# Key weights loaded second, behind one x tile; fold map built on GpSimd; first products and den/num products in parts; all engines' orders laid anew

## The chip, the cores and the metric

The kernel runs on one core of a Trainium2 chip. A core has TensorE (PE in the profile; PEld are its weight loads), VectorE (DVE), ScalarE (ACT), GpSimd (POOL) and SyncE (SP), which here only issues DMAs. The metric is the device time of one execution in microseconds, taken as the median of several runs.

## What is computed

x is 2048 tokens by 640, in bf16. First comes a linear attention of 32 heads of 20 columns, then an MLP, both with a layer norm ahead and a residual sum behind:

```python
qkv = (layernorm(x) @ wqkv)...            # q, k, v: (B, H, S, 20)
pq, pk = q @ w_phi[h], k @ w_phi[h]       # per head, 20 x 20
phi_q = concat([softmax(pq), softmax(-pq)])
phi_k = concat([softmax(pk), softmax(-pk)])
kv = einsum("bhsf,bhsd->bhfd", phi_k, v)
z  = phi_k.sum(over s)
o  = (phi_q @ kv) / (phi_q . z + 1e-6)
h  = x + o.reshape(B, S, D) @ wo
h2 = h + silu(layernorm(h) @ w1) @ w2     # w1: 640 x 1728, w2: 1728 x 640
```

## The kernel before

The tokens lie in 16 tiles of 128 (t = 0 to 15). The kernel has no loop that is seen in the trace: every step is a function `op_...` that issues a few instructions on one engine, and a long text, `ORDER` (lines 25 to 66), names the steps one after another. A word such as `vc.3.a` calls `op_vc(3, "a")`; the ending `.v`, `.a`, `.p` or `.s` names VectorE, ScalarE, GpSimd or the DMA queue of SyncE. Each engine carries out its own words strictly in the order of the text, and waits before each for the data and the buffers that it needs. So the text is at the same time the queue of each engine.

The steps, with the lines of the profile:

- Loads: `lx.a.b` (tiles a to b of x), `lk.a.b` (chunks of 128 rows of the key weights), `lv` (value weights), `lp` (w_phi), `lq.c` (query weights, transposed by DMA into the buffer of the key weights, once those have been read), `lo`, `l1`, `l2`, `lh` (wo, w1, w2). All but `lp` are issued by SyncE.
- Folding w_phi into the weights: `wt.c` transposes a chunk of the key weights on PE (L300), `wc.c` copies it out of PSUM; `mk` and `ph` (L187 to 193) spread w_phi over a mask to the block map `phb`; `fk.c` multiplies the two on PE (L315), `fc.c` copies out chunk c of the folded key weights `Wfk`. `gk` and `gc` do the same for the query weights `Wfq`.
- Layer norm of a tile: `st` (L258, L259, statistics on DVE), `rs` (L263, L264, the reciprocal root on GpSimd, for one or more tiles), `rm` (a bias for ScalarE), `xn` (the normalised tile: L275 on DVE, L280 on ACT). Then the transpose `XnT`: for tiles 0 to 3 `xt` on PE (L286) with the copy `xc`, for all others `xd`, a transposing DMA (L293).
- Key side: `kp` (L343, ten matmuls of the tile with `Wfk`), `ke` (L365, two exponentials on ACT), `kr` (L373 row sums and L376 reciprocal on DVE), `ka` (L381, the normalisation of 1280 columns on GpSimd; `ka.t.h` does half and `kb` the other half on DVE). Value side: `vp` (L343, ten matmuls) and `vc` (copy to `Vp`). `cc` (L403, 20 small matmuls) adds the tile to kv and z, which stay in one PSUM buffer up to `km` (L413).
- Query side, for groups of four tiles: `qp` (L423, ten or five matmuls of 512 columns) and `qe` (L433, exponentials).
- After `close`, per tile: `dp` (L457, numerator and denominator), `dw` (L470 to L477) and `dr` on DVE, `do` (L492, two halves, on DVE or GpSimd), `td` (transposing DMA to `ot`), `op` (L519, times wo), `oa` (L528, residual), `sq`, `sa`, `sr`, `hn` (second layer norm), `hd` (transposing DMA), `up` (L593, L603) and `ua` (SiLU), `yp` and `yh` (L639, L654), `yo`, `so` (output).
- `wm` is a matmul of zeros whose result nobody reads; eight stand ahead of the text, four more in it (L252).

PSUM gives four buffers, `mm`, for all products and PE transposes; kv holds one of them from the first `cc` to `km`. The exponentials `Ek` have eight buffers, the normalised tiles `xn` seven, the value tiles `Vp` ten.

Of the kernel before, what the change touches and what calls it, by code (L numbers as in the profile page):

```python
# [47 lines left out]
dw.8.v do.6.1.p do.6.0.p sr.2 td.6 op.9 hn.5 ua.0.2 sa.3 hn.2 dr.10 sa.4 hd.2 do.10.1.v dp.7 sr.4
dr.8 yp.0.0 oa.9 hd.5 dw.7.v sa.9 sq.9 do.8.0.p yp.0.1 sr.3 do.10.0.v sr.9 yh.0.0 dr.7 td.10 dp.11
yo.0 do.8.1.p yp.1.0 hn.4 dw.11.v hd.4 yp.1.1 td.8 hn.3 dr.11 op.6 hd.3 yo.1 dp.13 oa.6 op.8 dw.13.v  # L50
op.10 hn.9 up.1.1 oa.10 oa.8 dr.13 sa.8 sq.8 up.1.2 do.7.1.v do.11.1.p do.11.0.v sq.6 do.7.0.p sr.8
td.7 up.1.6 ua.1.2 do.13.1.p hn.8 td.11 ua.1.1 do.13.0.v dp.15 ua.1.6 so.0 up.1.3 dw.15.v td.13 hd.8
dp.12 ua.1.3 dr.15 op.7 hd.9 dw.12.v up.1.5 oa.7 dr.12 sa.7 sq.7 up.1.0 do.12.1.v do.15.0.p ua.1.5
sr.7 sa.6 hn.7 up.1.4 ua.1.0 sa.10 do.12.0.p sr.6 td.12 op.11 ua.1.4 op.13 oa.11 do.15.1.v yp.4.1
oa.13 td.15 hn.6 hd.6 yh.1.0 dp.14 yp.4.0 dw.14.v hd.7 yp.2.0 dr.14 do.14.1.v yo.4 op.15 up.2.2
oa.15 up.2.1 ua.2.2 sq.11 yp.2.1 op.12 up.2.4 oa.12 do.14.0.v sa.12 yo.2 sa.11 td.14 up.2.5 so.4
up.2.3 ua.2.5 ua.2.4 ua.2.1 up.2.0 ua.2.3 sq.10 up.2.6 ua.2.0 sq.15 yh.1.1 op.14 sq.13 sq.12 yp.3.1
oa.14 ua.2.6 sa.14 sq.14 sr.10 yp.7.1 sa.15 hn.10 sa.13 yp.3.0 sr.13 sr.11 yp.5.0 sr.15 hn.11 hd.11
sr.14 yp.5.1 sr.12 hn.14 hd.14 yp.9.0 yo.5 hn.13 so.2 hd.10 yp.9.1 hd.13 yo.3 yp.6.0 hn.12 so.1
hn.15 hd.15 yp.7.0 so.3 so.5 hd.12 yp.8.0 yh.2.1 yh.2.0 yo.9 yp.8.1 yo.7 yp.6.1 up.4.0 yo.6 so.6  # L60
up.3.0 ua.4.0 yo.8 so.8 up.4.2 so.7 so.9 up.4.3 up.3.6 ua.4.3 up.3.1 ua.3.6 ua.4.2 ua.3.0 up.3.3
up.3.2 up.4.1 ua.3.2 ua.3.1 up.3.5 ua.4.1 ua.3.3 up.3.4 ua.3.5 yp.15.1 ua.3.4 yh.4.0 yh.3.0 yp.15.0
yp.10.1 yo.15 so.15 yp.12.0 yp.14.1 yp.12.1 yp.14.0 yp.10.0 yo.14 so.14 yp.11.1 yo.10 yo.12 so.12
yh.3.1 yp.11.0 yq.13.0 yo.11 so.11 so.10 yq.13.1 yz.13.0 yz.13.1 sz.13.0.a sz.13.1.s
"""

@with_exitstack
def kernel(
# [103 lines left out]
    def tok(Xt, t):  # L172
        return Xt[:, :, (t % GT) * P : (t % GT + 1) * P]
# [10 lines left out]
            base=DH, pattern=[[-d, C], [DH, 8]], channel_multiplier=-1,  # L184
        )

    def op_ph():  # L187
        nc.vector.tensor_tensor(
            phb[:],
            phr[:].unsqueeze(2).to_broadcast([P, C, 8, DH]),  # L190
            mask5[:].unsqueeze(3).to_broadcast([P, C, 8, DH]),
            op=ALU.mult,
        )
# [56 lines left out]
    def op_wm(n=512, ps=None):  # L250
        ps = mm2() if ps is None else ps
        nc.tensor.matmul(ps[:, 0, 0:n], warm[:, 0:P], warm[:, 0:n], start=True, stop=True)  # L252
        return ps
# [82 lines left out]
            tl["gk", ce][:, :, 0:320].rearrange("p a (r k) -> p a r k", r=C),  # L336
        )

    def proj(t, W):
        ps = mm2()  # L340
        for half in range(2):
            for c in range(C):
                nc.tensor.matmul(  # L343
                    ps[:, half, 0:320], tok(XnT[t // GT], t)[:, c, :], W[:, c, half * 320 : (half + 1) * 320],
                    start=(c == 0), stop=(c == C - 1),
                )
# [4 lines left out]

    def op_vc(t, eng="a"):
        copy(
# [2 lines left out]
            tl["vp", t][:, :, 0:320].rearrange("p a (h f) -> p a h f", f=DH),  # L356
        )

    def op_kp(t):
        tl["kp", t] = proj(t, Wfk)  # L360

    def op_ke(t):
        Ek = first.tile([P, 2, D], BF16, name="Ek", bufs=8)
# [83 lines left out]
        for lo in (0, FH):  # L447
            dma(q, w2[lo : lo + FH, FC, :], B_w2[FC * P : F, :])

    def op_dp(t):  # L450
        g, i = t // GT, t % GT
        ps = [mm2(), mm2()]
        for s in range(2):
            for r in range(C):
                for a in range(2):
                    lo = 64 * a
                    nc.tensor.matmul(  # L457
                        ps[s][:, a, HQ[r] * 22 : (HQ[r] + 4) * 22],
                        EqT[g][lo : lo + 64, s, r, i * P : (i + 1) * P],
                        KVBD[lo : lo + 64, s, r, :, :].rearrange("p j c -> p (j c)"),  # L460
                        start=(r == 0),
                        stop=(r == C - 1),
                        skip_group_check=True,
                    )
# [251 lines left out]
```

## Time and profile before

| | |
|---|---|
| median of 3 runs | 243.91 us (243.8 to 245.86) |
| profiled execution | 244.62 us |
| its span, first to last instruction | 242.3 us |
| granted PE clock | 1.000 |
| ACT busy | 100.0 us (41%) |
| GpSimd busy | 85.5 us (35%) |
| DMA | 20.59 MB, mean 85 GB/s |

The span is what the profile shows; the execution's own time is 2.3 us longer, for what lies around the first and last instruction. "Busy" counts an engine's time inside instructions. A row of the timeline or the chain begins with its start in us from the beginning of the span and its length in us; a name such as `Ek<-Ek,Sk` is output and inputs; what stands in brackets at the end of a row is how long the engine sat idle ahead of it, and what released it. In a row by groups, "x16 | 23.3, 1453" is 16 instructions, 23.3 us in all, 1453 ns each. Matmuls are pipelined, so that rows that overlap are longer than what PE spends on them.

### The profile page before, as it was taken

Reading aid. Unit: us, or ns where it says so; the run is one execution under the profiler, and the core shown is the slowest. Engines: PE = TensorE matmul, PEld = TensorE weight load, DVE = VectorE, ACT = ScalarE, POOL = GpSimd, SP = SyncE. Lnnn points to the kernel's source line nnn. Section 1 sums busy time; section 2 is a strip of 40 time slices with the busy share of each in tenths; the row PEclk is TensorE's granted clock in tenths of the full one; section 3 lists DMA queues with packets and bytes.
Section 4 is the critical chain, followed back from the end, with each engine's and each line's share of the span. In section 5 each row is a group of like instructions: output and inputs, shape, how many; then the busy total and the mean of one; then the engine's idle time right before and its main releaser. Section 6 shows DMA issues by size and latency. Waiting matters only on the chain.

```text
span 242.3 us, 5172 instructions
## 1 busy us (share of the span) xinstructions
PE 233.0 (96%) x2144; PEld 150.0 (62%) x2160; DVE 142.2 (59%) x266; ACT 100.0 (41%) x149; POOL 85.5 (35%) x160
## 2 busy tenths in 40 slices
...
DMA packets 42806, 20.59 MB, mean 85 GB/s; under 512 B 34336, under 2 KB 42272, under 8 KB 42784
## 3 DMA queue, kind: packets, MB, share of 16 engines
...
q10 hardware_dynamic: 800, 0.16, 0.4%
...
## 4 chain that ended last, share of the span: by engine, by line
PE 79%; DVE 14%; DMA 4%; issue 1%; POOL 1%; ACT 0%; DVEq 0%; ACTq 0%
PE mm L639 24%; PE mm L593 23%; PE mm L519 9%; PE mm L423 8%; PE mm L343 7%; DVE Sk L373 4%; DVE stats L258 3%; PE mm L457 3%; DMA XnT<-xn 2%; DVE xn L275 2%; PE mm L403 2%; DMA X<-in_A_x_dram 1%; DVE Ek L381 1%; PE mm L654 1%; PE mm L603 1%
## 5 line engine op out<-in xcount | busy, mean ns | idle before, releaser
L639 PE MATMUL mm<-w,shT 128*128 128x320 bf16 (+2 forms) x415 | 58.2, 299 | 0.1
L593 PE MATMUL mm<-HnT,w 128*128 128x512 bf16 (+1 forms) x317 | 57.7, 336 | 0.4
L615 ACT ACTIVATE shT<-mm 128x1024 bf16<-128x1024 f32 (+2 forms) x29 | 27.0, 964 | 61.6 <-PE mm L593 55.9
L639 PEld LDWEIGHTS <-shT 128*128 128x128 bf16 x416 | 39.7, 98 | 17.4 <-issue 0.8
L593 PEld LDWEIGHTS <-w 128*128 128x128 bf16 x325 | 31.2, 98 | 23.8 <-issue 0.2
L343 PEld LDWEIGHTS <-XnT 128*128 128x128 bf16 x320 | 30.6, 98 | 15.5 <-DMA XnT<-xn 3.2
L662 DVE TENSOR_TENSOR ob<-mm,X 128x640 bf16<-128x640 f32 x15 | 12.1, 818 | 45.6 <-PE mm L639 36.9
L381 POOL TENSOR_TENSOR Ek<-Ek,Sk 128x1280 bf16<-128x1280 bf16 (+1 forms) x16 | 36.8, 2321 | 4.5 <-DVE Sk L376 4.2
L528 DVE SCALAR_TENSOR_TENSOR X<-mm,X 128x640 bf16<-128x640 f32 x16 | 13.0, 819 | 23.0 <-PE mm L519 22.8
L433 ACT ACTIVATE EqT<-mm 128x1024 bf16<-128x1024 f32 (+1 forms) x24 | 19.7, 880 | 13.7 <-PE mm L423 13.7
L343 PE MATMUL mm<-Wfk,XnT 128*128 128x320 bf16 x160 | 23.6, 300 | 1.4 <-DMA XnT<-xn 1.4
L343 PE MATMUL mm<-wv,XnT 128*128 128x320 bf16 x160 | 23.4, 299 | 1.4 <-DMA XnT<-xn 1.2
L365 ACT ACTIVATE Ek<-mm 128x640 bf16<-128x640 f32 x32 | 20.8, 711 | 9.3 <-PE mm L343 8.0
L373 DVE TENSOR_REDUCE Sk<-Ek 128x64 f32<-128x1280 bf16 x16 | 23.3, 1453 | 2.1 <-ACT Ek L365 2.1
L519 PE MATMUL mm<-wo,ot 128*128 128x320 bf16 x160 | 23.7, 300 | 0.0
L423 PE MATMUL mm<-XnT,Wfq 128*128 128x512 bf16 x93 | 23.1, 380 | 0.4
L541 POOL TENSOR_SCALAR HM<-HST 128x1 f32<-128x1 f32 x16 | 3.7, 232 | 52.2 <-DVE X L528 52.2
L536 ACT ACTIVATE sq<-X 128x640 bf16<-128x640 bf16 x16 | 11.8, 738 | 21.9 <-DVE X L528 20.0
L519 PEld LDWEIGHTS <-ot 128*128 128x128 bf16 x160 | 15.3, 98 | 6.9 <-issue 0.3
L492 POOL TENSOR_TENSOR o<-u,rd 128x320 bf16<-128x320 f32 x19 | 13.9, 742 | 13.8 <-DVE rd L486 7.7
L423 PEld LDWEIGHTS <-Wfq 128*128 128x128 bf16 x100 | 9.2, 98 | 10.0
L258 DVE BATCH_NORM_STATS2 stats<-X 128x6 f32<-128x320 bf16 x32 | 13.6, 467 | 3.0 <-DMA X<-in_A_x_dram 3.0
...
## 6 DMA issues: line engine op xcount, KB each, us to landing
...
```

Of the source, the lines that this page charges most:

```text
L258: nc.vector.bn_stats(stats[:, k, :], X[:, t, k * 320 : (k + 1) * 320])
L343: nc.tensor.matmul(ps[:, half, 0:320], tok(XnT[t // GT], t)[:, c, :], W[:, c, half * 320 : (half + 1) * 320], start=(c == 0), stop=(c == C ...
L365: nc.scalar.activation(Ek[:, s, :].rearrange("p (a n) -> p a n", a=2), tl["kp", t][:, :, 0:320], AF.Exp, scale=1.0 - 2.0 * s,)
L373: nc.vector.tensor_reduce(Sk[:], tl["ek", t][:].rearrange("p s (h f) -> p (s h) f", f=DH), axis=AX.X, op=ALU.add,)
L381: eng.tensor_tensor(Ek3, Ek3, tl["sk", t][:, lo:hi].unsqueeze(2).to_broadcast([P, hi - lo, DH]), op=ALU.mult,)
L423: nc.tensor.matmul(ps[:, k, :], Wfq[:, c, r * P : (r + 1) * P], XnT[g][:, c, :], start=(c == 0), stop=(c == C - 1),)
L433: nc.scalar.activation(E[:, s, rs[0] : rs[-1] + 1, :], tl["qp", g, i][:, 0 : len(rs), :], AF.Exp, scale=1.0 - 2.0 * s,)
L492: (nc.vector if eng == "v" else nc.gpsimd).tensor_tensor(tl["o", t][:, a * 320 : (a + 1) * 320].rearrange("p (h f) -> p h f", f=DH), tl["u ...
L519: nc.tensor.matmul(ps[:, half, 0:320], tl["ot", t][:, c, :], wo[:, c, half * 320 : (half + 1) * 320], start=(c == 0), stop=(c == C - 1),)
L593: nc.tensor.matmul(ps[:, i * W : (i + 1) * W], w1[:, c, fc * P : (fc + 1) * P], HnT[g][:, c, 0:W], start=(c == 0), stop=(c == C - 1), skip ...
L615: nc.scalar.activation(sh[:, a:b], tl["up", g, k][:, 0 : b - a], AF.Silu)
L639: nc.tensor.matmul(ps, shT[g][:, fc * W + i * P : fc * W + (i + 1) * P], w2[:, fc, a:b], start=first and fc == 0, stop=last and fc == FC - ...
```

## The change

- The loads begin with one tile of x (tile 3) in place of two; the key weights follow in the order 2, 1, 4, 0, then tile 2 of x, then key chunk 3. All loads of x are issued ahead of the first `xd`; `lo`, most of `l2`, `l1` and `lq` have other places.
- `ph` runs on GpSimd, ahead of `rs.3`.
- `kp` and `vp` can be issued in parts, over chunks lo to hi of the 640 rows: for tiles 2 and 3 in two parts each.
- `dp` is issued in halves, for s = 0 and s = 1, and takes one PSUM buffer each.
- Six warm-up matmuls ahead of the text in place of eight, two in it in place of four.
- The order of all words is another. All sixteen `st` stand ahead of the first `kr`. All sixteen `ka` run whole on GpSimd; there is no `kb`. All sixteen `vc` are on ACT (before, three on DVE), `xn` is on ACT for four tiles (before, two), `fc` on ACT for all five chunks. `qp.1.0` stands ahead of the last `cc`. Behind `close`, 23 half tiles of `do` are on GpSimd (before, 19).

The diff, with the order up to the words behind `close`, and its last line:

```diff
-lp.a lx.2.4.s ta lk.0.1.s lk.1.2.s mk lk.3.4.s lk.2.3.s lk.4.5.s lx.1.2.s lx.0.1.s st.3 lv.3.5.s
-lx.4.8.s st.2 wm.512 wm.256 wt.1 lv.0.3.s wt.3 wc.1.a ph rs.2.2 wt.0 wc.3.a wt.2 wc.0.v fk.1 wt.4
-wc.2.v fc.1.a fk.0 xn.2.v lq.2 fk.2 wc.4.v fc.0.a fk.3 xn.3.v fk.4 fc.2.a fc.3.v xt.3 lq.4 fc.4.a
-wm.256 xt.2 xc.3.v xc.2.a st.0 wm.512 kp.3 lq.3 st.1 rs.0 kp.2 lq.1 xn.0.v rs.1 st.5 lx.8.12.s xt.0
-ke.2 vp.3 xn.1.v st.4 xc.0.a vp.2 st.7 vc.3.a rs.4.2 st.6 xt.1 vc.2.a vp.0 xc.1.a xn.5.v rs.6.2 kr.2
-xd.5 gk.2 vc.0.a kp.0 mo gc.2.a ke.3 xn.6.v vp.1 xn.4.v ka.2.p xd.6 st.9 ke.0 kp.5 st.10 xd.4 xn.7.v
-gk.3 lx.12.16.s ke.5 st.8 vp.5 xd.7 st.11 gc.3.a kp.1 lq.0 vc.5.a kr.0 rs.8.4 vp.4 rm.8 st.15 ka.0.p
-vp.6 vc.4.a st.12 ke.1 kp.7 st.13 xn.8.a mc kp.4 xn.9.v vc.6.a xd.8 xn.11.v vc.1.a st.14 gk.1 xd.9
-ke.4 kp.6 kr.3 rs.12.4 gc.1.a l2.0.4.s vp.7 xd.11 ke.7 xn.12.v ka.3.p kr.5 vp.8 l1.0.s vc.7.a ke.6
-gk.0 xn.15.v vp.9 rm.14 xn.10.v ka.5.p gc.0.a kr.4 vc.8.a gk.4 kp.9 gc.4.a xn.13.v ka.4.p kr.6 xd.13
-cc.0 cc.2 ke.9 cc.3 l2.4.8.s cc.5 xd.10 kp.11 vc.9.a ka.6.p kr.9 xn.14.a lh.s qp.0.2 ke.11 xd.14
-kr.7 kp.8 l1.2.s xd.12 qp.0.0 ke.8 kr.1 ka.7.p xd.15 qe.0.2 vp.13 kr.11 qe.0.0 l2.8.13.s lo.s ka.1.p
-l1.1.s kp.13 kr.8 kp.14 ka.11.p cc.6 ke.14 cc.7 cc.1 ka.8.h cc.4 vc.13.a kr.14 kp.10 ke.13 kp.12
-ke.10 kr.13 ka.14.p kp.15 ke.12 kr.10 qp.0.1 ka.9.p ke.15 kb.10 vp.14 qe.0.1 kb.8 ka.10.h kr.15
-vp.11 ka.13.p vc.14.a vp.15 vc.11.v kr.12 ka.15.p vp.10 vc.15.a vp.12 vc.10.v ka.12.p cc.13 vc.12.v
-cc.10 cc.9 cc.8 cc.14 cc.15 cc.11 cc.12 qp.1.2 km.0 close km.1 dp.1 qe.1.2 qp.1.0 dw.1.v dp.0 qe.1.0
-dr.1 qp.1.1 dw.0.v do.1.0.p dp.3 qe.1.1 dr.0 qp.3.0 dw.3.v do.0.1.p do.1.1.p do.0.0.p td.1 dp.4
-qe.3.0 dr.3 qp.2.1 dw.4.v td.0 dp.5 do.3.1.v qe.2.1 qp.2.0 do.3.0.v dr.4 dw.5.v do.4.1.p do.4.0.p
-op.1 qe.2.0 td.4 dr.5 op.0 oa.1 td.3 sa.1 dp.2 oa.0 do.5.0.p qp.2.2 dw.2.v sa.0 sq.0 do.5.1.p qp.3.2
-qe.2.2 sr.0 td.5 op.4 qe.3.2 dr.2 do.2.1.v do.2.0.p sq.1 dp.9 oa.4 td.2 op.3 sr.1 hn.0 hd.0 hn.1
...
-yh.3.1 yp.11.0 yq.13.0 yo.11 so.11 so.10 yq.13.1 yz.13.0 yz.13.1 sz.13.0.a sz.13.1.s
+lp.a lx.3.4.s ta lk.2.3.s lk.1.2.s mk lk.4.5.s lk.0.1.s ph.p lx.2.3.s st.3 lk.3.4.s wt.2 lx.0.2.s
+lv.0.3.s wt.1 rs.3 wc.2.v lv.3.5.s wt.4 wc.1.v wt.0 lx.4.8.s mc wc.4.a fk.2 xn.3.v lx.8.12.s fk.1
+wc.0.v fc.2.a st.2 wm.512 fk.0 fc.1.a wt.3 xt.3 fc.0.a lq.1 wc.3.v fk.4 rs.2 xc.3.v wm.256 fk.3
+fc.4.a kp.3.0.3 xn.2.v fc.3.a lq.2 st.0 xt.2 kp.3.3.5 xc.2.a lx.12.16.s st.1 vp.3.0.3 ke.3 kp.2.0.3
+rs.0.2 kp.2.3.5 xn.0.v vp.2.0.3 ke.2 xn.1.v st.5 xt.0 vp.2.3.5 xc.0.a st.4 vp.3.3.5 xt.1 kp.0 st.6
+xc.1.a rs.4.2 vc.2.a vp.1 xn.5.v xn.4.v xd.5 st.7 vp.0 vc.1.a st.8 xd.4 rs.6.2 vc.3.a gk.2 st.11
+vc.0.a rm.7 kp.1 lq.0 ke.0 st.9 lq.4 vp.5 ke.1 st.10 xn.6.v vp.4 xn.7.a rs.8.4 st.12 xd.6 vc.5.a
+st.13 kp.5 mo vc.4.a xd.7 gc.2.a st.14 kp.4 ke.5 lo.s rm.9 xn.11.v st.15 gk.4 xn.9.a gk.0 kr.3 kp.6
+rs.12.4 gc.4.a xd.9 ke.4 vp.6 rm.14 lq.3 rm.13 xn.8.v ke.6 ka.3.p kr.1 vp.7 xd.11 gc.0.a gk.1 xd.8
+xn.12.v vc.7.a ka.1.p kp.7 kr.2 xn.14.a xd.12 vc.6.a vp.9 xn.13.a xn.15.v ka.2.p kr.0 gc.1.a kp.9
+xd.13 vc.9.a ke.7 vp.11 xd.15 xn.10.v ka.0.p kr.5 l2.4.8.s cc.1 l1.2.s cc.3 vc.11.a l2.0.4.s cc.2
+kr.6 xd.14 ke.9 gk.3 ka.5.p kp.8 gc.3.a lh.s vp.13 kr.7 ke.8 l1.1.s ka.6.p xd.10 kp.12 vc.13.a kr.4
+vp.12 ka.7.p kr.9 kp.15 vc.12.a ke.12 ka.4.p kp.13 kr.8 kp.11 ka.9.p kr.12 cc.5 cc.6 ke.15 cc.7 cc.0
+cc.4 ka.12.p ke.11 kr.15 kp.14 ke.13 vp.15 kr.11 ka.15.p ke.14 vp.14 vc.15.a kr.14 vp.8 ka.8.p kp.10
+vc.8.a kr.13 ka.14.p qp.0.0 ke.10 vc.14.a kr.10 qp.0.2 ka.13.p qe.0.0 vp.10 qe.0.2 ka.11.p qp.1.0
+vc.10.a qp.0.1 ka.10.p qe.1.0 cc.15 qe.0.1 cc.9 cc.12 cc.11 cc.14 cc.13 cc.8 cc.10 qp.1.2 km.0 close
+km.1 dp.1.0 qe.1.2 dp.1.1 qp.1.1 dw.1.v dp.0.0 qe.1.1 dp.0.1 dr.1 qp.2.1 dw.0.v dp.3.0 qe.2.1 dp.3.1
+dr.0 qp.3.0 dw.3.v do.0.1.p do.0.0.p td.0 dp.5.1 qe.3.0 dp.5.0 dr.3 qp.2.0 dw.5.v l1.0.s do.3.0.p
+do.1.0.p do.3.1.p do.1.1.p dp.4.0 td.3 qe.2.0 dp.4.1 dr.5 op.0 dw.4.v do.5.0.p td.1 do.5.1.p qp.2.2
+oa.0 dp.2.1 qe.2.2 dp.2.0 dr.4 qp.3.2 dw.2.v do.4.1.p sq.0 do.4.0.p op.1 qe.3.2 sa.0 td.4 sr.0
...
+yp.11.1 yh.3.1 yq.13.0 yo.11 yo.10 so.11 so.10 yq.13.1 yz.13.0 yz.13.1 sz.13.0.s sz.13.1.a
@@ 
             base=DH, pattern=[[-d, C], [DH, 8]], channel_multiplier=-1,
         )
 
-    def op_ph():
-        nc.vector.tensor_tensor(
+    def op_ph(eng="v"):
+        (nc.vector if eng == "v" else nc.gpsimd).tensor_tensor(
             phb[:],
             phr[:].unsqueeze(2).to_broadcast([P, C, 8, DH]),
             mask5[:].unsqueeze(3).to_broadcast([P, C, 8, DH]),
@@ 
             tl["gk", ce][:, :, 0:320].rearrange("p a (r k) -> p a r k", r=C),
         )
 
-    def proj(t, W):
-        ps = mm2()
+    def proj(key, t, W, lo, hi):
+        if lo == 0:
+            tl[key, t] = mm2()
+        ps = tl[key, t]
         for half in range(2):
-            for c in range(C):
+            for c in range(lo, hi):
                 nc.tensor.matmul(
                     ps[:, half, 0:320], tok(XnT[t // GT], t)[:, c, :], W[:, c, half * 320 : (half + 1) * 320],
                     start=(c == 0), stop=(c == C - 1),
                 )
-        return ps
-
-    def op_vp(t):
-        tl["vp", t] = proj(t, wv)
+
+    def op_vp(t, lo=0, hi=C):
+        proj("vp", t, wv, lo, hi)
 
     def op_vc(t, eng="a"):
         copy(
@@ 
             tl["vp", t][:, :, 0:320].rearrange("p a (h f) -> p a h f", f=DH),
         )
 
-    def op_kp(t):
-        tl["kp", t] = proj(t, Wfk)
+    def op_kp(t, lo=0, hi=C):
+        proj("kp", t, Wfk, lo, hi)
 
     def op_ke(t):
         Ek = first.tile([P, 2, D], BF16, name="Ek", bufs=8)
@@ 
         for lo in (0, FH):
             dma(q, w2[lo : lo + FH, FC, :], B_w2[FC * P : F, :])
 
-    def op_dp(t):
+    def op_dp(t, s):
         g, i = t // GT, t % GT
-        ps = [mm2(), mm2()]
-        for s in range(2):
-            for r in range(C):
-                for a in range(2):
-                    lo = 64 * a
-                    nc.tensor.matmul(
-                        ps[s][:, a, HQ[r] * 22 : (HQ[r] + 4) * 22],
-                        EqT[g][lo : lo + 64, s, r, i * P : (i + 1) * P],
-                        KVBD[lo : lo + 64, s, r, :, :].rearrange("p j c -> p (j c)"),
-                        start=(r == 0),
-                        stop=(r == C - 1),
-                        skip_group_check=True,
-                    )
-        tl["dp", t] = [p[:, :, 0:352].rearrange("p a (h c) -> p a h c", c=22) for p in ps]
+        ps = mm2()
+        for r in range(C):
+            for a in range(2):
+                lo = 64 * a
+                nc.tensor.matmul(
+                    ps[:, a, HQ[r] * 22 : (HQ[r] + 4) * 22],
+                    EqT[g][lo : lo + 64, s, r, i * P : (i + 1) * P],
+                    KVBD[lo : lo + 64, s, r, :, :].rearrange("p j c -> p (j c)"),
+                    start=(r == 0),
+                    stop=(r == C - 1),
+                    skip_group_check=True,
+                )
+        tl.setdefault(("dp", t), {})[s] = ps[:, :, 0:352].rearrange("p a (h c) -> p a h c", c=22)
 
     def op_dw(t, eng="v"):
         A = tl["dp", t]
@@ 
     ops = {k[3:]: f for k, f in locals().items() if k.startswith("op_")}
     with tc.manual_schedule(engines={PE, SP, POOL, DVE, ACT}):
         ps = None
-        for i in range(8):
+        for i in range(6):
             ps = op_wm(512, ps)
         for word in ORDER.split():
             name, *args = word.split(".")
```

More of the change, by code (lines that the diff above doesn't have):

```diff
@@ L42 @@
-dr.1 qp.1.1 dw.0.v do.1.0.p dp.3 qe.1.1 dr.0 qp.3.0 dw.3.v do.0.1.p do.1.1.p do.0.0.p td.1 dp.4
-qe.3.0 dr.3 qp.2.1 dw.4.v td.0 dp.5 do.3.1.v qe.2.1 qp.2.0 do.3.0.v dr.4 dw.5.v do.4.1.p do.4.0.p
-op.1 qe.2.0 td.4 dr.5 op.0 oa.1 td.3 sa.1 dp.2 oa.0 do.5.0.p qp.2.2 dw.2.v sa.0 sq.0 do.5.1.p qp.3.2
-qe.2.2 sr.0 td.5 op.4 qe.3.2 dr.2 do.2.1.v do.2.0.p sq.1 dp.9 oa.4 td.2 op.3 sr.1 hn.0 hd.0 hn.1
-qp.3.1 oa.3 hd.1 dw.9.v sq.3 op.5 qe.3.1 op.2 oa.5 sa.5 dp.10 oa.2 up.0.0 dr.9 dw.10.v do.9.0.p sa.2
-up.0.3 ua.0.0 do.9.1.v dp.6 sq.4 td.9 up.0.1 dw.6.v sq.5 ua.0.3 sr.5 sq.2 dp.8 dr.6 ua.0.1 up.0.2
@@ L48 @@
[L48 to L63, printed above, removed]
-yh.3.1 yp.11.0 yq.13.0 yo.11 so.11 so.10 yq.13.1 yz.13.0 yz.13.1 sz.13.0.a sz.13.1.s
+lp.a lx.3.4.s ta lk.2.3.s lk.1.2.s mk lk.4.5.s lk.0.1.s ph.p lx.2.3.s st.3 lk.3.4.s wt.2 lx.0.2.s
@@ new lines @@
+dr.0 qp.3.0 dw.3.v do.0.1.p do.0.0.p td.0 dp.5.1 qe.3.0 dp.5.0 dr.3 qp.2.0 dw.5.v l1.0.s do.3.0.p
+do.1.0.p do.3.1.p do.1.1.p dp.4.0 td.3 qe.2.0 dp.4.1 dr.5 op.0 dw.4.v do.5.0.p td.1 do.5.1.p qp.2.2
+oa.0 dp.2.1 qe.2.2 dp.2.0 dr.4 qp.3.2 dw.2.v do.4.1.p sq.0 do.4.0.p op.1 qe.3.2 sa.0 td.4 sr.0
+dp.9.1 dr.2 dp.9.0 oa.1 op.3 td.5 hn.0 sa.1 sq.1 dw.9.v do.2.1.p hd.0 qp.3.1 sr.1 hn.1 op.4 oa.3
+qe.3.1 hd.1 sa.3 op.5 do.2.0.p oa.4 td.2 sq.4 dp.10.0 dp.10.1 up.0.1 dw.10.v l2.8.13.s op.2 dr.9
+ua.0.1 dr.10 do.9.1.p oa.5 do.10.0.p up.0.3 oa.2 do.9.0.v dp.6.1 ua.0.3 dp.6.0 dp.8.1 sq.3 dw.6.v
```

17 lines of the change are left out of this document (added).

## The prediction

> **What bounds the kernel now.** I read the page's busy line first, then busy time by stretch, the list of waits, and the chain of waits.
>
> ```profile
> PE 233.0 (96%) x2144; PEld 150.0 (62%) x2160; DVE 142.2 (59%) x266; ACT 100.0 (41%) x149; POOL 85.5 (35%) x160
> 0.00:72.46 72.46, 67.23 (x781) 47.01 (x784) 62.87 (x106) 44.85 (x69) 49.62 (x61) 1.00 0.69 173
> 72.46:239.02 166.56, 165.77 (x1364) 102.97 (x1378) 79.06 (x160) 55.17 (x80) 35.91 (x99) 1.00 0.26 47
> 239.02:242.30 3.28, 0.00 (x0) 0.00 (x0) 0.27 (x1) 0.00 (x0) 0.00 (x0) 1.00 0.17 50
> ```
>
> The columns of the last three rows are the stretch, its length, then PE, PEld, DVE, ACT and POOL busy. I cut at 72.46, where the last kv product (`cc`) ends. Behind it PE lacks 0.8 us in 166.6: there is nothing to win there, only to lose. Ahead of it PE lacks 5.2, and part of its 67.2 is warm-up. So what the change can win lies ahead of 72.46. The two longest waits there, for a transpose `XnT`, are quoted further down; the next one:
>
> ```profile
> PE mm L403 <- DVE Vp L158: 0.6, 1, 0.6
> ```
>
> ```profile
> 0.79 3.37 DMA X<-in_A_x_dram
> ...
> 17.60 1.41 DVE Sk L373
> ...
> 24.90 5.96 DMA XnT<-xn
> ...
> 33.80 0.32 PE mm L315 x6
> ...
> 40.18 1.36 PE mm L343 x10
> 41.53 1.65 PE mm L403 x80
> ...
> 69.59 2.86 PE mm L403 x140
> ...
> 73.63 0.50 PE mm L457 x20
> ...
> 85.18 2.27 PE mm L423 x10
> ```
>
> The chain (start, length, what) runs through DVE up to 24.9, over one slow transpose to 30.9, then over PE, over DVE and GpSimd again from about 53 to 69.6, and over PE to the end. It also gives PE's prices: a `kp` or `vp` 1.36, a `gk` or a PE transpose 0.32, a `cc` 1.65/4 = 0.41, a `dp` 0.5, a `qp` of ten 2.27 (of five 1.14).
>
> **The new order, engine by engine.** Everything is carried to one point, the end of the last `cc`, since what PE does behind it stays the same but for one `qp`, which moves ahead of it.
>
> DVE first, since all 16 `st` now stand ahead of the first `kr`, and every `ka` waits for a `kr`.
>
> ```profile
> L258 DVE BATCH_NORM_STATS2 stats<-X 128x6 f32<-128x320 bf16 x32 | 13.6, 467 | 3.0 <-DMA X<-in_A_x_dram 3.0
> L259 DVE BATCH_NORM_AGGREGATE MV<-stats 128x2 f32<-128x12 f32 x16 | 3.3, 208 | 0.6
> L158 DVE COPY wTk<-mm 128x640 bf16<-128x640 bf16 x3 | 1.4, 482 | 0.0
> L373 DVE TENSOR_REDUCE Sk<-Ek 128x64 f32<-128x1280 bf16 x16 | 23.3, 1453 | 2.1 <-ACT Ek L365 2.1
> L376 DVE RECIPROCAL Sk<-Sk 128x64 f32<-128x64 f32 x16 | 8.8, 553 | 0.6
> L188 DVE TENSOR_TENSOR phb<-phr,mask 128x800 bf16<-128x800 bf16 x1 | 1.0, 952 | 0.0
> L158 DVE CAST Wfk<-mm 128x640 bf16<-128x640 f32 x1 | 0.8, 819 | 0.0
> ```
>
> ```profile
> L275 DVE TENSOR_SCALAR xn<-X,MV,RS x8: 394/444/2469, 8.1 to 24.5; 128x640 bf16<-128x640 bf16 x8
> ```
>
> A `st` is 16.9/16 = 1.06, a copy 0.48, a normalisation `xn` 0.44 (median), a `kr` 1.45 + 0.55 = 2.0. Trial on the old queue: 8 `st`, `ph`, 4 copies, 1 cast and 5 `xn` give 14.35; it took 17.60 - 4.16 = 13.4, since neighbours overlap, so I scale by 0.94. The new queue ahead of the first `kr`: 16 `st` 16.9, 5 copies 2.4, 8 `xn` 3.5: 22.8, scaled 21.4. `ph` (0.95), the cast `fc.3` and, later, three casts of `Vp` and two half tiles `kb` have left DVE.
>
> Start: one x tile, half the bytes, in place of two.
>
> ```profile
> 5.35 0.45 PE L300 MATMUL mm<-ident,wk 128*128 128x128 bf16 x5
> ```
>
> Between the landing at 4.16 and this first transpose two key chunks land, as many bytes as the two tiles, in 1.2. The one tile lands between 3.6 (if half of that goes) and 4.16 (if it is all latency); I take 3.9.
>
> Waits that this order adds. GpSimd does `ph` as soon as its operand has landed, and `rs.3` stands behind it; `xn.3` on DVE waits for `rs.3`, with `wc.0`, `st.2` and the rest queued behind.
>
> ```profile
> phr<-in_A_w_phi_dram ACTq DMA_DIRECT2D x1, 25.0 KB, 3.7
> ```
>
> ```profile
> L381 POOL TENSOR_TENSOR Ek<-Ek,Sk x16: 1267/2356/2933, 19.7 to 69.0; 128x1280 bf16<-128x1280 bf16 x14, 128x640 bf16<-128x640 bf16 x2
> ```
>
> ```profile
> 15.39 0.23 POOL L263 TENSOR_SCALAR RS<-MV 128x2 f32<-128x2 f32 x1 [1.79 <-DVE MV L259]
> 15.71 0.71 POOL L264 TENSOR_TENSOR RS<-RS,nhalf 128x2 f32<-128x2 f32 x1
> ...
> 38.30 7.15 POOL L381 TENSOR_TENSOR Ek<-Ek,Sk 128x1280 bf16<-128x1280 bf16 x3
> ```
>
> The operand is there at 0.79 + 3.7 = 4.5. `ph` on GpSimd is not in the trace; its 800 elements cost between DVE's 0.95 and a full `ka`'s 2.36; on the line through the half tile (1.27) and the full one (2.36) 1.54, which I take: 6.05. `rs.3` takes at most what the form for two tiles takes, 1.03 (15.39 to 16.42): 7.1. DVE is there at 3.9 + 1.06 + 0.96 = 5.9, so it waits 1.2. Next, `rs.0.2` takes tiles 0 and 1 together and waits for `st.1`, and `xn.0` stands right behind `st.1`: 1.03 and a hand-over, 1.1 more, with `rs.4.2` queued behind it. First `kr`: 3.9 + 21.4 + 2.3 = 27.6.
>
> GpSimd: `kr.3` to 29.6, `xn.8` to 30.0, then 16 full `ka` back to back. Three in a row took 7.15, so 2.38 each: 38.1, to 68.1. Three more `xn` stand among them. That the two engines shut each other out is in the rows:
>
> ```profile
> 19.73 2.61 POOL L381 TENSOR_TENSOR Ek<-Ek,Sk 128x1280 bf16<-128x1280 bf16 x1
> 20.06 2.47 DVE L275 TENSOR_SCALAR xn<-X,MV,RS 128x640 bf16<-128x640 bf16 x1
> ```
>
> An `xn` of 0.4 lasted 2.47, until the `ka` was over. The Trainium skill (SBUF — State Buffer, Terms, on the shared port pair) says the same: an exclusive lock held for the whole instruction, the loser fully blocked. By that rule `ph` would hold up only an `xn`, and none is due while it runs; the sum stays. Each `xn` thus holds up the next `ka` by 0.4: 1.2 in all, so GpSimd ends at 69.3 and the last `cc` could end at 69.8.
>
> PE: the first product needs `xc.3`. DVE: `xn.3` to 7.5, `wc.0`, `st.2`, `wc.3`, `xc.3` (0.48 + 1.06 + 0.48 + 0.48, scaled 2.4) to 9.9. So 10.0 in place of 10.58:
>
> ```profile
> 10.58 2.88 PE L343 MATMUL mm<-Wfk,XnT 128*128 128x320 bf16 x20
> ...
> 26.66 2.89 PE L343 MATMUL mm<-wv,XnT 128*128 128x320 bf16 x20 [1.15 <-DMA XnT<-xn]
> ...
> 30.91 2.89 PE L343 MATMUL mm<-Wfk,XnT 128*128 128x320 bf16 x20 [1.35 <-DMA XnT<-xn]
> ```
>
> From there to the last `cc`: 32 products 43.5, 5 `gk` 1.6, 3 transposes 1.0, 16 `cc` 6.6, three `qp` of ten and one of five 7.9: 60.6. The same count for the old order (two transposes, two `qp` of ten and one of five) is 58.0, with its waits (1.15 + 1.35 + 0.6) 61.1, against 61.9 measured, so 0.8 of small ones goes on top: 10.0 + 61.4 = 71.4. PE is later than GpSimd by 1.6, so PE sets the point.
>
> Does PE run dense? The transposes it waited for: the old `xd.7` (issued at 24.9) stood behind a 640 KB load of x, which now stands ahead of all `xd`. `xd.5` follows `xn.5`: DVE has done 7 `st`, 5 copies and 5 `xn` (12.0, scaled 11.3) and both waits by 17.5, say 17.7. Landing is 4.3 median:
>
> ```profile
> XnT<-xn SPq DMA_TRANSPOSE x12, 4.3
> ot<-o SPq DMA_TRANSPOSE x16, 2.6
> ```
>
> so it is there at 22.0; PE, with eight products, three transposes and a `gk` (12.2) behind 10.0, comes to `vp.5` at 22.2. `xd.4`, 1.2 later, is needed 1.36 later. No slack, but no queue ahead either: 0 to 1.7 us of wait (at 6.0, the longest landing), I take 0.1. `xd.9` now stands behind the 800 KB of `wo` on SP, and its `xn.9` on ACT behind `ke.5`, which needs `kp.5` (26.3); PE comes to `vp.9` five products and three `gk` later, at 34.1, so 7.8 for ACT's work (some 3) and a landing of 4.3. The weight loads now ahead of `xd.14` and `xd.10` are covered by the seven products, a `gk` and five `cc` ahead of `kp.14` (11.9); if that cover is gone, PE waits there, with `qp` behind. ACT takes on about 4 us (three casts of `Vp`, two `xn`), with 27 free. For all these I put 0.3, so the last `cc` ends at 71.7. The split products add no instruction; `dp` in halves takes one buffer at a time, a gain of nothing where PE didn't wait. Two warm-ups fewer at the head cover a shorter start.
>
> Sum: 71.7, then what stood behind 72.45 in the old span (169.85) less the one `qp` (2.27): 239.3, which is 3.0 under 242.3. By the profiled execution 244.62 - 3.0 = 241.6; the median of the runs stood 0.7 lower, at 243.91, so 240.9.
>
> **Rivals.** *Slow start of the matmuls.* Rows first:
>
> ```profile
> 1.24 4.23 PE L252 MATMUL mm<-warm 128*128 128x512 bf16 x10 [1.24 <-DVE warm L130]
> ...
> 6.03 1.01 PE L300 MATMUL mm<-ident,wk 128*128 128x128 bf16 x15 [0.23 <-DMA wk<-in_A_wqkv_dram]
> ```
>
> A warm-up of 512 columns takes 0.42, a `qp` matmul of 512 columns 0.227: PE starts at half pace, though the granted clock reads 1.00. By 6.03 fifteen of 128 columns take 1.01: full pace, with 4.1 us of warm-ups ahead of the first transpose. Six warm-ups end at 1.24 + 2.5 = 3.8, and PE then has transposes, small products and holes up to 10.0. If the pace is still half there, it takes another 4.1 us of products to lift it, at a loss of 2.05: 242.95 (two such spells: 245.0). For it: the shorter head. Against: the old trace holds its pace from 5.35 to 10.58 with small work too. The Trainium skill (TensorE: Matmul & The Clock Gate, Part 1) has the gate opening after a busy window of about 3.4 us, and Part 4 has transposes not counted as busy in the same way, which speaks for this rival; the rows leave it open. Chance 0.13.
>
> *The cover behind `close` is missed.* `qp.1.0` filled 2.27 there. The new order reaches `op.0` after five `dp` and four `qp`, 2.5 + 9.1 = 11.6. Its `ot` needs `dp.0` (3.3), DVE's `dw` and `dr`, two `do` and a transpose of 2.6:
>
> ```profile
> 77.08 0.29 DVE L470 RECIPROCAL w<-mm 128x32 f32<-128x32 f32 x1
> ...
> 79.70 0.36 DVE L470 RECIPROCAL w<-mm 128x32 f32<-128x32 f32 x1
> ...
> 79.84 2.10 POOL L492 TENSOR_TENSOR o<-u,rd 128x320 bf16<-128x320 f32 x3 [1.65 <-DVE rd L486]
> ```
>
> 3.3 + 2.6 + 1.4 + 2.6 = 9.9, so 1.7 are spare. If that fails, the stage gives back at most what the filler covered, 2.27: 243.1. Chance 0.12.
>
> *The transposes come late again*, with another queue ahead: 2.5 of wait stay, 243.3. Chance 0.07.
>
> *GpSimd becomes the bound: slower.* Its `ka` start at 30.0, ten later than now, and nothing is left out between them. If a tile costs 2.93, the longest row, the last ends at 30.0 + 46.9 + 1.2 = 78.1, the last `cc` at 78.5; against 72.45 + 2.27 = 74.7, the point of no gain, 3.8 late: 247.7. It decides against the change from (74.7 - 0.4 - 31.2)/16 = 2.69 a tile. For it: it has little slack, 1.6 against PE. Against: `kr` ran beside the three at 2.38. Chance 0.14.
>
> **The numbers.** Forecast 240.9, chance 0.54, its own range 239.0 (no new waits, an earlier x tile, `ph` at DVE's price: 1.9 better) to 242.4 (1.5 of wait at the transposes). A measurement here tells about 1% (2.4 us) from no change. Under 241.5: most of the forecast's case, 0.5. Over 246.3: most of the GpSimd case, 0.13. Between: 0.37, the other three and the rest of these two. The range goes from 239.0 to 245.3: it takes in the three middle cases and leaves out most of the slower one and the forecast's lower edge.
>
> **What would show it.** `ph` at about 4.5 for 1.5 on GpSimd and `xn.3` waiting for it; the first product at 10.0; no PE wait over 0.5 between 20 and 35; the first `ka` near 30, sixteen to about 69; the last `cc` near 71.7 with a fourth `qp` ahead of it; PE dense behind. Wrong: products at 0.27 a matmul after 10.0, PE waiting for `ka` at the end, or for `ot` behind `close`.

## The result, and the profile after

The changed kernel takes 240.93 us (median of 4 runs, 240.85 to 240.95), the one before, run beside it, 243.87. The ratio is 0.9853, with a 95% interval from 0.9804 to 0.9902: about 1.5% faster. The two medians alone differ by 2.9 us, 1.2%, which lies inside that interval. The forecast was 240.9.

Busy line of the page, and busy time by stretch (stretch, length, then PE, PEld, DVE, ACT and GpSimd), cut at the first product of a tile with folded weights and at the end of the last `cc`:

```profile
PE 232.8 (97%) x2140; PEld 151.5 (63%) x2156; DVE 130.6 (55%) x254; ACT 104.4 (44%) x154; POOL 90.8 (38%) x167
0.00:11.18 11.18, 8.93 (x69) 6.25 (x69) 5.22 (x14) 4.54 (x7) 6.39 (x24) 1.00 0.82 260
11.18:71.47 60.29, 60.24 (x724) 43.26 (x722) 48.56 (x85) 45.70 (x70) 45.31 (x40) 1.00 0.60 134
71.47:235.70 164.23, 163.27 (x1349) 101.76 (x1365) 76.08 (x155) 54.19 (x78) 39.07 (x103) 1.00 0.27 58
```

The span is 239.0, 3.3 less. The middle row is the whole result: from the first product at 11.18 to the last `cc` at 71.47 PE lacks 0.05 us. Before, it lacked 3.4 from 10.58 to 72.46 and had one query product less to do. From the last `cc` to the end of the span it is 239.0 - 71.47 = 167.53; the sum had 169.85 - 2.27 = 167.58. So the change in the last 164 us of PE's work is nothing, and all the gain lies where the prediction looked for it.

The start went otherwise than forecast. Timeline of PE and of DVE:

```profile
5.71 1.78 PE L302 MATMUL mm<-ident,wk 128*128 128x128 bf16 x15 [0.95 <-DMA wk<-in_A_wqkv_dram]
7.28 1.41 PE L317 MATMUL mm<-phb,wTk 128*128 128x140 bf16 x12
...
10.01 0.44 PE L288 MATMUL mm<-ident,xn 128*128 128x128 bf16 x5
...
11.18 0.98 PE L347 MATMUL mm<-Wfk,XnT 128*128 128x320 bf16 x6
...
68.22 3.25 PE L406 MATMUL mm<-Vp,Ek 128*64 128x84 bf16 x160
```

```profile
L160 DVE COPY wTk<-mm 128x640 bf16<-128x640 bf16 x4 | 2.0, 492 | 2.9 <-PE mm L302 2.9
```

The same fifteen transposes that took 1.01 us before take 1.78 here: PE is at half pace, and it stays there through the folds until about 10: the trace's record of the granted clock has its first entry, a step to full clock, at 9.97 us, and that of the kernel before at 5.34. In the second row DVE waits 2.9 us in all for PE's transposes of the key weights (0.37, 1.18, 0.16 and 1.16), ahead of its four copies. So the first product comes 0.6 *later* than before, at 11.18, not 0.6 earlier.

On GpSimd the block map and the sixteen `ka`:

```profile
3.72 1.52 POOL L190 TENSOR_TENSOR phb<-phr,mask 128x800 bf16<-128x800 bf16 x1 [1.17 <-DMA phr<-in_A_w_phi_dram]
...
31.65 9.55 POOL L384 TENSOR_TENSOR Ek<-Ek,Sk 128x1280 bf16<-128x1280 bf16 x4
...
50.42 18.56 POOL L384 TENSOR_TENSOR Ek<-Ek,Sk 128x1280 bf16<-128x1280 bf16 x8
```

The last `ka` ends at 50.42 + 18.56 = 68.98. The last of eight `cc`, which reads it, starts some 0.4 ahead of PE's end of them, at about 71.06: 2.1 to spare. `cc.4` and `cc.2`, earlier, have 1.6 and 1.3.

### The profile page after: what moved, and what is told of

Read it like the earlier page. It is cut to its first block, busy times and chain, and to the rows that moved or that the text cites. A ratio compares the mean times of both kernels' runs of the same rounds, so it can differ in the third digit from the quotient of the medians.

```text
span 239.0 us, 5196 instructions
## 1 busy us (share of the span) xinstructions
PE 232.8 (97%) x2140; PEld 151.5 (63%) x2156; DVE 130.6 (55%) x254; ACT 104.4 (44%) x154; POOL 90.8 (38%) x167
## 4 chain that ended last, share of the span: by engine, by line
PE 95%; DMA 2%; ACT 1%; issue 1%; SPq 0%; DVE 0%
PE mm L641 24%; PE mm L595 24%; PE mm L347 18%; PE mm L426 9%; PE mm L521 9%; PE mm L459 3%; PE mm L406 3%; PE mm L317 2%; DMA wk<-in_A_wqkv_dram 2%; PE mm L605 1%; PE mm L656 1%; PE mm L302 1%; ACT EqT L436 1%; PE mm L288 0%; SPq L220 0%
## 5 line engine op out<-in xcount | busy, mean ns | idle before, releaser
L595 PE MATMUL mm<-HnT,w 128*128 128x512 bf16 (+1 forms) x316 | 58.3, 335 | 0.4
L617 ACT ACTIVATE shT<-mm 128x1024 bf16<-128x1024 f32 (+2 forms) x29 | 27.6, 964 | 59.2 <-PE mm L595 53.8
L384 POOL TENSOR_TENSOR Ek<-Ek,Sk 128x1280 bf16<-128x1280 bf16 x16 | 37.3, 2371 | 0.0
L494 POOL TENSOR_TENSOR o<-u,rd 128x320 bf16<-128x320 f32 x23 | 16.7, 748 | 24.0 <-DVE rd L488 11.8
L368 ACT ACTIVATE Ek<-mm 128x640 bf16<-128x640 f32 x32 | 20.3, 718 | 4.4 <-PE mm L406 2.7
L560 DVE TENSOR_SCALAR hn<-X,HM 128x640 bf16<-128x640 bf16 x16 | 7.1, 456 | 15.1 <-POOL HM L554 15.1
```

What stands on the lines that cost most here:

```text
L368: nc.scalar.activation(Ek[:, s, :].rearrange("p (a n) -> p a n", a=2), tl["kp", t][:, :, 0:320], AF.Exp, scale=1.0 - 2.0 * s,)
L384: eng.tensor_tensor(Ek3, Ek3, tl["sk", t][:, lo:hi].unsqueeze(2).to_broadcast([P, hi - lo, DH]), op=ALU.mult,)
L494: (nc.vector if eng == "v" else nc.gpsimd).tensor_tensor(tl["o", t][:, a * 320 : (a + 1) * 320].rearrange("p (h f) -> p h f", f=DH), tl["u ...
L595: nc.tensor.matmul(ps[:, i * W : (i + 1) * W], w1[:, c, fc * P : (fc + 1) * P], HnT[g][:, c, 0:W], start=(c == 0), stop=(c == C - 1), skip ...
L617: nc.scalar.activation(sh[:, a:b], tl["up", g, k][:, 0 : b - a], AF.Silu)
```

## The experiments

Three questions were put to the chip. Is PE or the `ka` chain what sets the end? Which part of the change brought the gain? What did the slow start cost, and why was it slow? Every experiment was timed beside the kernel before; across these groups of runs its median lay between 244.25 and 244.34, so I compare ratios. One hundredth of ratio is 2.4 us; the changed kernel stands at 0.9853.

**GpSimd later by half a tile, and by two tiles.** A scratch tile `zz`, set to zero at the start, is multiplied by itself on GpSimd ahead of the first `ka`:

```diff
+    def op_zz(n):
+        nc.gpsimd.tensor_tensor(zz[:, 0:n], zz[:, 0:n], zz[:, 0:n], op=ALU.mult)
 # ORDER
-... ke.6 ka.3.p kr.1 ...
+... ke.6 zz.640 ka.3.p kr.1 ...
+... ke.6 zz.1280 zz.1280 ka.3.p kr.1 ...
```

> The changed kernel with one extra multiplication of 640 columns on a scratch tile on GpSimd, right ahead of the first ka: all sixteen ka come 1.27 later. Theory PE: the cc find their ka with 1.3 to spare at cc.2, 1.6 at cc.4 and 2.1 at cc.10, so the time stays, 240.9 to 241.0. Theory GpSimd: 1.3 more, 242.2.

> The same with two extra multiplications of 1280 columns: all ka come 4.75 later. Theory PE: the spare 1.3 goes first, then one for one: 3.3 to 3.5 more, 244.2 to 244.4, with PE waiting for Ek at cc.2. Theory GpSimd: the full 4.75 more, 245.7. If PE had more cover than the trace shows (later cc could catch up), it would be under 3.0.

Half a tile (it took 1.32): 240.87 us, ratio 0.9853 (0.9813 to 0.9892), no change. In the profiled run the first `ka` came at 32.64, 1.0 later than in the changed kernel. So the `ka` chain has that much to spare, and PE sets the end. Two tiles: 245.7 us, 1.0048 (1.0024 to 1.0073), 4.8 more by ratio. By its time alone this is the GpSimd theory's number, against the half tile. Its timeline of PE shows why:

```profile
40.59 0.95 PE L410 MATMUL mm<-Vp,Ek 128*64 128x84 bf16 x40 [1.95 <-POOL Ek L388]
42.90 0.91 PE L410 MATMUL mm<-Vp,Ek 128*64 128x84 bf16 x20 [1.36 <-POOL Ek L388]
43.75 0.78 PE L321 MATMUL mm<-phb,wk 128*128 128x140 bf16 x6
44.32 2.52 PE L351 MATMUL mm<-Wfk,XnT 128*128 128x320 bf16 x10
46.68 1.52 PE L351 MATMUL mm<-wv,XnT 128*128 128x320 bf16 x10
```

PE waits 1.95 + 1.36 = 3.3 for `Ek`, in two pieces among the first three `cc`, as long in all as expected. Then the next ten matmuls take 2.52 in place of 1.52: PE has dropped to half pace. The busy time by stretch shows it; the granted clock is the third figure from the end:

```profile
42.93:46.34 3.41, 3.41 (x34) 2.50 (x35) 3.34 (x5) 0.92 (x2) 3.41 (x2) 0.50 1.08 391
```

In 3.41 us at half clock PE gets 1.7 us less done, and the first product stood 0.6 earlier in this run, at 10.57: 3.3 + 1.7 - 0.6 = 4.4 of the 4.5 by which the span is longer. Only the wait was in the expectation. GpSimd doesn't set the end here either: the last `ka` ends at 73.16, and the last `cc` starts at about 75.6. Of the ten runs seven have a mean clock of 0.993, which is one such stretch, one has 0.986, and two have 1.000; those two took 244.63 and 244.90, near the 244.2 to 244.4 of the PE theory.

**The products of tiles 2 and 3 whole.**

```diff
-... kp.3.0.3 ... xt.2 kp.3.3.5 ... vp.3.0.3 ... kp.2.0.3 kp.2.3.5 ... vp.2.0.3 ... vp.2.3.5 ... vp.3.3.5
+... xt.2 kp.3 ... kp.2 ... vp.2 ... vp.3
```

> The changed kernel with the products of tiles 2 and 3 whole again, each at the place of its second part. Theory PE: PE sets the end from the first product on. kp.3 must now wait for the last folded chunk (about 12.1 in place of 11.18), one transpose (0.3) goes ahead of it, and xt.0 comes due a little earlier than its tile: 0.6 to 0.9 more, 241.5 to 241.8. Theory GpSimd: the chain of ka from 31.6 to 69.0 sets the end and PE only fits: no change, 240.9.

241.72 us, 0.9879 (0.9835 to 0.9923): 0.6 more by ratio, which the intervals can't tell from nothing, and 1.0 in the span. The first product is at 11.86, 0.7 later, and PE then waits 0.37 for `xn.0`; the last `cc` ends at 72.5, 1.0 later. In this trace, what delays PE's first product comes out at the end, as the PE theory has it.

**One part alone: the loads of x early in the kernel before.**

```diff
-... lv.0.3.s ... lq.1 ... lx.8.12.s xt.0 ... gk.3 lx.12.16.s ke.5 ...
+... lv.0.3.s lx.8.12.s lx.12.16.s ... lq.1 ... xt.0 ... gk.3 ke.5 ...
```

> The kernel before with one part of the change alone: the loads of x tiles 8 to 15 issued right behind the first part of the value weights, ahead of all transposes. Theory of the transposes: PE's two waits for XnT (1.15 and 1.35) go, and with them DVE's later waits for Ek (0.57 and 1.54), which only followed from PE being late; the last cc comes 1.5 to 2.1 earlier, the time falls by as much (about 242.0 beside 243.9). Rival: DVE has no room (56.4 busy of the 61.9 from the first product to the last cc), so the chain over DVE and GpSimd behind 53 us eats the gain: at most 0.5 better, 243.4.

**Another alone: three value copies on ACT in the kernel before.**

```diff
-... vc.11.v ... vc.10.v ... vc.12.v ...
+... vc.11.a ... vc.10.a ... vc.12.a ...
```

> The kernel before with another part alone: the copies of the value products of tiles 10, 11 and 12 on ACT in place of DVE. DVE's chain at the end of the stage gets 2.2 shorter, of which 0.7 ahead of the last kr. Theory of the transposes and the end: PE's last waits (0.2 and 0.6) go, ka.12 ends 0.7 earlier: 0.6 to 1.0 better, 243.0. Rival: GpSimd, which runs ka without a hole from 57 on, sets the end: 0.3 or less.

**Both of them in the kernel before.**

```diff
-... lv.0.3.s ... lx.8.12.s ... lx.12.16.s ... vc.11.v ... vc.10.v ... vc.12.v ...
+... lv.0.3.s lx.8.12.s lx.12.16.s ... vc.11.a ... vc.10.a ... vc.12.a ...
```

> The kernel before with both parts, the early loads of x and the three copies on ACT. If the waits add up: 2.1 to 2.9 better, 241.0 to 241.8, most of what the whole change brings. If either part only uncovers the other's bound: no better than the better of the two alone by more than 0.2.

The loads alone: 242.86 us, 0.9946 (0.9929 to 0.9963), 1.3 better. The copies alone: 243.11, 0.9957 (0.9942 to 0.9971), 1.0 better. Both: 241.53, 0.9891 (0.9877 to 0.9906), 2.7 better. Within the intervals they add up, so neither hid behind the other. The rival of the loads, that DVE has no room, falls. These rows are from the lists of waits, of the kernel before and of the one with early loads:

```profile
DVE Sk L373 <- ACT Ek L365: 2.1, 2, 1.5
```

```profile
PE mm L342 <- DMA XnT<-xn: 1.1, 2, 0.8
...
DVE Sk L372 <- ACT Ek L364: 0.4, 1, 0.4
```

DVE's waits for `Ek` fell from 2.1 to 0.4 when PE came earlier; they had been the consequence of PE's lateness. PE still waits 1.1 for transposes. In the profiled run the last `cc` ends 1.95 earlier, at 70.51, inside the 1.5 to 2.1 expected; by ratio the gain lies between 0.9 and 1.7. With the copies on ACT the last `cc` waits for `ka.12`, not for a copy, here in the kernel with both:

```profile
69.28 0.57 PE L402 MATMUL mm<-Vp,Ek 128*64 128x84 bf16 x20 [0.23 <-POOL Ek L380]
```

So two edits of a few words bring 2.7 us, where the whole new order brings 3.6 by its ratio (1.47% of 244.3) and 2.9 by the medians. No run divides the rest among the other parts.

**The query product back behind `close`.**

```diff
-... ka.11.p qp.1.0 vc.10.a qp.0.1 ka.10.p qe.1.0 ... dp.1.1 qp.1.1 dw.1.v dp.0.0 ...
+... ka.11.p vc.10.a qp.0.1 ka.10.p ... dp.1.1 qp.1.0 qp.1.1 dw.1.v qe.1.0 dp.0.0 ...
```

> The changed kernel with the query product qp.1.0 moved back behind close. Theory PE: the work is the same and only its place changes; PE comes to the last cc 2.27 earlier and finds ka.10, which had 2.1 to spare, 0.2 late: 240.9 to 241.2. Rival, the cover: behind close the extra product fills small holes before op and dp: up to 0.5 better. If the last cc were really waiting for GpSimd, it would be 1.0 or more slower.

240.76 us, 0.9853 (0.9829 to 0.9877): no change, with a wait of 0.2 for the last `Ek` in the list of waits. Its place shows no worth, neither as cover behind `close` nor ahead of the last `cc`; the interval, 0.6 us to either side, doesn't exclude the 0.5 of the rival.

**The block map on DVE again.**

```diff
-... lk.0.1.s ph.p lx.2.3.s st.3 lk.3.4.s ...
+... lk.0.1.s lx.2.3.s st.3 ph lk.3.4.s ...
```

> The changed kernel with the block map ph on DVE again, right behind st.3. Theory PE with the slow start: DVE sits idle anyway from 4.4 on, waiting for PE's transposes at half pace (0.37 and 1.18), and 0.95 of ph fits in but for some 0.5 that delays wc.2; wc.1 and all behind it wait for wt.1 as before: 240.8 to 241.0. Theory as predicted, DVE dense from the first tile on: ph costs 0.95 on DVE and saves the 1.2 that xn.3 waits for rs.3, so 0.2 to 0.3 better, 240.7. If moving ph off DVE was worth its full duration: 241.9.

240.34 us, 0.9835 (0.9797 to 0.9872); its runs go from 239.48 to 241.37, wider than the difference from the changed kernel, so whether it gains the predicted 0.2 to 0.3 stays open. What falls is that taking `ph` off DVE was worth 0.95: DVE waits for PE's transposes there anyway. With `ph` among them those waits came to 1.7 in place of 2.9.

**A longer warm-up.** Two more matmuls of zeros at the head, and two in PE's hole behind the first transpose:

```diff
-        for i in range(6):
+        for i in range(8):
 # ORDER
-... wt.2 lx.0.2.s ...
+... wt.2 wm.512 wm.512 lx.0.2.s ...
```

> The changed kernel with more warm-up: eight matmuls of zeros at the head in place of six, and two more between the first transpose of the key weights and the second, where PE stood idle from 4.75 to 5.71. Theory of the pace: in the changed kernel PE works at half pace up to about 10.0 because the head is too short (fifteen transposes took 1.78 us, before 1.01), which puts the first product at 11.18. With the pace up by 5.7 the transposes and folds need some 2 us less, the first product comes between 9.7 and 10.2, and since PE runs dense from there, the time falls by 1.0 to 1.5 (239.4 to 239.9). Rival: the loads set the first product, the pace does not matter: within 0.3 of 240.9.

239.52 us, 0.98 (0.9757 to 0.9843): 1.3 better than the changed kernel by ratio, 1.7 in the span. The timeline of PE and the stretches:

```profile
5.67 1.25 PE L301 MATMUL mm<-ident,wk 128*128 128x128 bf16 x15
...
9.52 0.98 PE L346 MATMUL mm<-Wfk,XnT 128*128 128x320 bf16 x6
```

```profile
9.52:69.80 60.28, 60.23 (x724) 43.26 (x722) 48.68 (x85) 45.68 (x70) 45.31 (x40) 1.00 0.62 144
```

The step to full clock comes at 5.30 in place of 9.97. The transposes are shorter again, the first product is 1.66 earlier, and from there to the last `cc` PE takes 60.28, as it took 60.29: the 1.66 goes through to the end whole. By its own interval, 1.0 us to either side, this version can't be told from the changed kernel; the two further versions with matmuls in the hole, below, have narrower ones and come out alike.

**Only the two in the hole.** The head stays at six.

```diff
-... wt.2 lx.0.2.s ...
+... wt.2 wm.512 wm.512 lx.0.2.s ...
```

> The changed kernel with the head of six as it is, and only the two matmuls of zeros between the first transpose of the key weights and the second. If the pace is lifted by PE being steadily at work, whatever the work, then 1.24 to about 5.5 is one spell again (the six at the head, five transposes from 4.05, two fillers), the pace is up by 6, and the time is that of the longer warm-up, 239.3 to 239.8. If the five transposes do not count as work, the spell breaks at 4.0, the pace comes up only at about 9, and the time stays at 240.6 to 241.0.

239.81 us, 0.9812 (0.9796 to 0.9828), 1.0 better than the changed kernel.

```profile
4.12 0.71 PE L301 MATMUL mm<-ident,wk 128*128 128x128 bf16 x5
4.62 0.70 PE L253 MATMUL mm<-warm 128*128 128x512 bf16 x2
5.58 1.30 PE L301 MATMUL mm<-ident,wk 128*128 128x128 bf16 x15 [0.26 <-DMA wk<-in_A_wqkv_dram]
...
9.48 0.98 PE L346 MATMUL mm<-Wfk,XnT 128*128 128x320 bf16 x6
...
12.51 0.97 PE L346 MATMUL mm<-wv,XnT 128*128 128x320 bf16 x6 [1.23 <-DMA wv<-in_A_wqkv_dram]
```

That is at the upper edge of the range for steady work of any kind, and in this trace the step to full clock comes at 4.82. The fillers had run for only 0.2 by then, so it is the times that speak for them, not this trace: with the hole filled, eleven of twelve runs (this version, the longer warm-up, and the last one below) took 240.36 or less; with it open, seventeen of twenty (the changed kernel, half a tile, the query product back, the block map on DVE, a head of two) took 240.59 or more. The last row shows what can be late next: with the first product at 9.5, PE waited 1.23 for the value weights, which stand behind the key weights and x tiles 3, 2, 0 and 1, and landed 8.1 after their issue. In the longer warm-up they took 5.6, and PE had no such wait.

**A head of two.**

```diff
-        for i in range(6):
+        for i in range(2):
```

> The changed kernel with two warm-up matmuls at the head in place of six. Theory of the pace: PE reaches full pace only after a spell of steady matmuls, and with the head gone that spell falls on the first products: they start at 11.2 to 11.8 and some 2 to 4 us of them go at half pace (0.27 a matmul), 1.0 to 2.5 more than the changed kernel, 241.9 to 243.4. Rival: transposes and folds lift the pace as well as matmuls of zeros do, so four fewer change nothing beyond what six already cost: within 0.3 of 240.9.

240.88 us, 0.9864 (0.9849 to 0.988): no change, the rival is right.

```profile
5.94 1.78 PE L302 MATMUL mm<-ident,wk 128*128 128x128 bf16 x15 [1.11 <-DMA wk<-in_A_wqkv_dram]
...
9.70 0.44 PE L302 MATMUL mm<-ident,wk 128*128 128x128 bf16 x5
```

From 5.94 PE works steadily at transposes and folds, and the step to full clock comes 3.7 later, at 9.64, about where it comes with six at the head (9.97). Here a head of six that ended in a hole was worth no more than one of two.

**Longer warm-up and no wait for the roots of tiles 0 and 1.**

```diff
-... st.0 ... st.1 ... rs.0.2 ... xn.0.v
+... st.0 rs.0 ... st.1 rs.1 ... xn.0.v
```

> The changed kernel with the longer warm-up (as in the first experiment, 239.5) and with the reciprocal roots of tiles 0 and 1 each by itself, right behind their st, so that DVE no longer waits 1.16 for them ahead of xn.0. Theory PE: PE has no wait there, so DVE's wait costs nothing and the time is that of the longer warm-up alone, 239.4 to 239.7. Rival: DVE's lateness carries through kr and ka to the end: 0.5 to 1.1 better than 239.5.

239.44 us, 0.9803 (0.9789 to 0.9818): that of the longer warm-up. The first product is at 9.79, and PE again takes 60.28 from there to the last `cc`. DVE's wait ahead of `xn.0` costs nothing, since PE has no wait there.

## Why the prediction held, and where it didn't

The time was met to 0.1 us, but that is luck, since two errors cancel: a first product 1.2 too early, and 1.4 too much for what PE does from there to the last `cc`. What bounds the kernel, and where the gain lies, was right.

- *What bounds the kernel, and that PE sets the point.* Right. PE dense from the first product on, GpSimd with little room: no wait for half a tile more, 3.3 for two.
- *The first product at 10.0.* Wrong: 11.18. The step that failed is the sum of DVE's queue at the start, which took DVE as dense but for `rs.3`, and with it the sentence that two warm-ups fewer cover a shorter start. DVE waited 2.9 for PE's transposes, and those went at half pace; lifting the pace gave 1.66 back. Two terms erred the other way, the x tile by 0.6 and the wait for `rs.3` by 1.2 (below): 10.0 - 0.6 - 1.2 + 2.9 = 11.1.
- *The rival of the slow start*, given 0.13, is what happened, but not with its price. It had the lost time on the products (2.05); it fell on the transposes and folds ahead of them, which were themselves enough to lift the pace by the time the products began.
- *`ph`.* 1.54 forecast, 1.52 measured. But its operand was there by 3.72, not at 4.5, so `rs.3` was done at 6.24 (5.67 + 0.57) and nobody waited for it; the 1.2 of that wait was not there. The 1.1 ahead of `xn.0` was (1.16), and cost nothing.
- *The first x tile.* Statistics started at 3.29, outside the bounds of 3.6 to 4.16: half the bytes saved more than half of what the next bytes took.
- *61.4 from the first product to the last `cc`, and 0.3 of new waits.* Measured 60.29. The count of instructions alone (60.6) was right to 0.4. Of the 0.8 "of small ones", carried over from the old order, some 0.3 was waits of that order (PE lacked 3.4 in all, the sum named 3.1); the rest was PE busy for 58.4 where the count had 58.0. Neither came back in the new order.
- *The transposes.* No wait, as the sum had it. They landed in 2.6 in the median, not 4.3; the longest took 6.5, but PE waited for none, and the rival that they come late again fell.

```profile
XnT<-xn SPq DMA_TRANSPOSE x12, 2.6
```

- *First `ka` at 30.0, sixteen to 69.3.* The first came at 31.65, since DVE was late from the start (with the longer warm-up it came at 30.13); the last ended at 68.98. Four took 9.55 (2.39 each) with the `xn` among them, the last eight 2.32 each: the 0.4 that each `xn` was to cost the next `ka` came to about 0.07. An `xn` among them lasted 0.38 to 0.50, not 2.47; that DVE's `kr` and `xn` together take about as long as a `ka`, so that each `xn` comes due just as a `ka` ends, would explain it, but no run tried another beat.
- *GpSimd as the bound*, the slower rival: no tile came near 2.69, the point from which it decides. It was right that little room was left.
- *The cover behind `close`*: not missed, and moving it back changed nothing that the runs can tell.
